# Sigmoid attention and skip-MoE on one core: v's shared rows loaded once, the first expert chosen a batch earlier, gates behind the count, an aligned loop

## The chip, the cores and the metric

The kernel runs on one core of a Trainium2 chip. The metric is the device time of one execution in microseconds. The engines are TensorE (PE; PEld is its weight load), VectorE (DVE), ScalarE (ACT), GpSimd (POOL) and SyncE (SP, which issues most of the DMAs). Every engine works through its own instructions in the order in which they were written; semaphores make it wait for others.

## The reference

q, k and v have the shape (8, 12, 448, 64): B=8 batches, 12 heads, 448 positions, 64 elements a head. Attention's output is the input of a mixture of experts with N = 3584 tokens of 768 elements, 8 experts and a hidden width of 1024. Tokens whose skip score is not above zero pass unchanged.

```python
scores = scale * np.matmul(q, k.transpose(0, 1, 3, 2)) - np.log(S)
attn = 1.0 / (1.0 + np.exp(-scores))
x = np.matmul(attn, v).transpose(0, 2, 1, 3).reshape(B * S, H * D)
do_compute = x @ w_skip > 0
xc = x[do_compute]
logits = xc @ w_gate
e_idx = np.argmax(logits, axis=1)              # one expert a token
probs = softmax(logits)                        # with 1e-9 in the denominator
gate_w = probs[np.arange(len(xc)), e_idx]
for e in range(8):                             # mask: the tokens of expert e
    h = np.maximum(xc[mask] @ w1[e], 0.0)
    y[mask] = gate_w[mask, None] * (h @ w2[e])
out = x.copy()
out[do_compute] = xc + y
```

## The kernel before

**Attention** is 48 steps (b, hp): eight batches by six pairs of heads; n counts the steps. A step has four chunks c: three of 448 columns and, for c=3, one of 224. For each chunk PE makes the scores (s<-x, line 217), ACT the sigmoid (at<-s, line 237), and PE the product with v (pa<-at,v, line 245). The products stand two chunks behind the scores in PE's order, so values(n, c=3) stands in step n+1 at c=1.

**What feeds it.** Every second step loads the k and q of two steps (load_kq, line 177), and v for two steps (load_v, line 191). v's rows come in seven chunks of 64. The upper 64 partitions of a v tile hold chunks 0 to 3, the lower 64 chunks 3 to 6: chunk 3 is loaded twice. k and q are loaded once with a shift; four POOL copies (other_part, line 184) at c=0 of every even step n make the shifted part for steps n+2 and n+3. DVE's two transposes (prep, line 202) at c=0 and c=1 turn them into the x of the next step. For the first step alone, kq_first is loaded with both parts by DMA, on SP and ACT.

**What leaves it.** Step n's sum is added and turned by DVE (lines 255 and 260) and stored by SP (line 268).

**Routing** of batch b-1 runs beside the attention of batch b: logits at hp=0, route at hp=1, the six gate instructions (lines 352 to 358) at hp=2, c=1, ahead of the second transpose. route_count at hp=2, c=3 counts the tokens before each token (matmuls pc, then DVE lines 375 to 389) and leaves four puts, kept in a list `due`: POOL scatters of 112 tokens' records into each expert's list (line 394). They are taken from the list at hp=3 (two), and at hp=4 between the kq copies (two).

**The first expert.** choose_first, at step (B-5, hp=3), takes the expert with most tokens so far (three batches counted). From step W0 = N-26 on, its weights come in 28 pieces through seven buffers wr (line 456), how_many pieces in each step. One step later wsplit makes of each piece a high part on DVE (wh, line 465) and a low part on POOL (wl, line 466).

**The experts.** Behind attention the first 256 tokens of the first expert are computed (names b_ph, b_py), and DVE works out a plan of the remaining blocks. A runtime loop (line 1493) reads the kind of the next block and branches into one of four arms, which stand in the order FULL, FEW, HALF, SPLIT. FEW takes up to 32 tokens and HALF up to 64, with raw weights; SPLIT is a full block that also splits the next expert's raw weights. While a block runs, SP loads the raw weights of the next expert (lines 1176 and 1185). Each pass ends with a POOL scatter of its tokens (line 550). In the trace 14 passes ran, the first a SPLIT and the last a FEW.

The order of the instructions is written by hand (tc.manual_schedule). The chosen first expert and the plan are decided at run time from the data.

Of the kernel before, what the change touches and what calls it, by code (L numbers as in the profile page):

```python
# [23 lines left out]
def kernel(  # L24
# [161 lines left out]
    def load_v(b, hp, n):  # L186

        x = io.tile([P, 2 * n, NV, D], F32, tag="v", name=f"v_{b}_{hp}", bufs=2)
        a = v[b, 2 * hp : 2 * (hp + n)]
        for m in range(2):  # L190
            nc.sync.dma_start(
                x[m * D : (m + 1) * D].rearrange("p h c d -> p h (c d)"),
                a.rearrange("h (p c) d -> p h (c d)", c=NR7)[:, :, 3 * m * D : (3 * m + NV) * D],
            )
        return x

    def prep(b, hp, t, xs=None):
# [10 lines left out]
    def scores(b, hp, c, xs):  # L208

        sc = new_s(f"s_{b}_{hp}_{c}")
        for m in range(2):
            first, qs = (4 * m + c, slice(0, S)) if c < 3 else (3, slice(m * HQ, (m + 1) * HQ))
            for j in range(2):
                r = slice(j * D, (j + 1) * D)
                nc.tensor.matmul(  # L217
                    sc[m * D : (m + 1) * D, j, : qs.stop - qs.start],
                    xs[r, 0, first::NR7],
                    xs[r, 1, qs],  # L220
                    start=True,
                    stop=True,
                )
        return sc
# [135 lines left out]
    def route_count(b, rec):  # L360
# [5 lines left out]
        for s in range(1, NC + 1):  # L366
# [13 lines left out]
        )  # L380

        nc.vector.scalar_tensor_tensor(
            pos, pos, -OOB, hb[:, :NC], op0=ALU.add, op1=ALU.mult
        )
        nc.vector.tensor_tensor(base, base, pc[:, n:m], op=ALU.add)
        sel = sm.tile([P, NC], F32, tag="sel", name=f"sel_{b}", bufs=1)
# [176 lines left out]

    W0 = N - 26
    how_many = (1, 1, 1, 1, 1, 2) * 4
    order = tc.manual_schedule()
# [5 lines left out]
    for n in range(2):  # L572
        for h, eng in enumerate((nc.sync, nc.scalar)):
            load_kq(kq0, 0, 0, slice(0, 1), range(ND), (n,), (h,), eng)
    kq = {0: new_kq(0, 0)}
    load_kq(kq[0], 0, 0, slice(1, 2), range(1))

    warm = const.tile([P, 1], F32, name="warm")
    nc.scalar.activation(warm, bias, AF.Sigmoid)
    vs = {0: load_v(0, 0, 2)}  # L580
    kq[1] = new_kq(*steps[2])
# [44 lines left out]
    xts, lts, rts, sgs = {}, {}, {}, {}  # L626
    wrs = []

# [16 lines left out]
    for n, (b, hp) in enumerate(steps):  # L645
# [39 lines left out]
        for c in range(4):  # L685
# [3 lines left out]
            if c == 0 and n % 2 == 0 and n + 2 < N:  # L689
                for g in range(2):  # L690
                    other_part(kq[n // 2 + 1], g)
                    if due and hp == 4 and b < B - 1:
                        due.pop(0)()
            if c == 0 and nxt:
# [8 lines left out]
            if c == 1:  # L703
                if hp == 2 and b > 0:
                    gates(pb, rts[pb])
                if nxt:
# [4 lines left out]
                if n % 2 == 0 and n + 2 < N:  # L711
                    vs[n // 2 + 1] = load_v(*steps[n + 2], 2)
            if c == 1 and n == N - 2:

# [7 lines left out]
            if c == 2:  # L722
                if hp == 3 and b == B - 5:
                    choose_first()
# [6 lines left out]

            if due and hp == 3 and (c % 2 if b < B - 1 else c < 2):
                due.pop(0)()
# [9 lines left out]
            if c == 3 and hp == 2 and b > 0:  # L743
                due = route_count(pb, rts[pb][0])
                if b == B - 1:
                    for _ in range(2):
                        due.pop(0)()
# [3 lines left out]
            if c == 3 and hp == 2 and b > 0:  # L751
                if pb == B - 2:
                    close_first()
        wrs = wrs_next
        xs = xs_next
# [345 lines left out]
    for j in range(2):  # L1101
        gemm2(j, hh0, hl0, py)
    turn0(1)
    for j in range(2, NK2 - 3):
        gemm2(j, hh0, hl0, py)
# [418 lines left out]
```

## Time and profile before

| what | us |
|---|---|
| runs | 537.68, 531.07, 534.7; median 534.7 |
| profiled execution | 538.86, with a span of 537.2 |
| before the first score of PE | 0 to 7.6 |
| attention | 7.6 to 285.9 |
| first expert's first two blocks (b0, b1) | 285.9 to 325.2 |
| first pass of the loop | 325.2 to 347.9 |
| thirteen more passes | 347.9 to 521.4 |
| behind PE's last matmul | 521.4 to 537.2 |

A row of a view is either a group (engine, line, operation, tiles, count, busy time, mean of one, idle time ahead) or a single run of instructions (start, duration, engine, line, operation, in brackets the idle time ahead and what ended it). An arrow `out<-in` names the tile written and the tiles read. A row of the waits names the waiting engine and line, what it waited for, and then the total, the times and the longest. A row of the chain has start, duration, engine, line.

### The profile page before, as it was taken

The page shows a single profiled execution, that of the slowest core. Times are in us where ns is not written, and L with a number is a line of the kernel's source. Part 1 is how long each engine was busy: PE and PEld are TensorE (multiplying, and loading weights), DVE is VectorE, ACT ScalarE, POOL GpSimd, SP SyncE. Part 2 cuts the span into 40 slices and gives each one's busy share as a digit, 9 for nine tenths or more (in the row PEclk, how much of TensorE's full clock was granted, in tenths as well). Part 3 has the DMA queues.
Part 4 walks back from the last instruction along what each step waited for, and adds up shares of the span by engine and source line. Part 5 has one row for each costly group of instructions (what it writes and reads, how often), then busy time and mean ns, then how long its engine had stood idle before and what let it go on. Part 6 is the DMA issues. An engine that isn't in the chain of part 4 may idle for free.

```text
span 537.2 us, 15241 instructions
## 1 busy us (share of the span) xinstructions
PE 506.3 (94%) x4985; PEld 337.0 (63%) x4986; DVE 296.9 (55%) x732; ACT 274.0 (51%) x483; POOL 259.5 (48%) x413
## 2 busy tenths in 40 slices
PE   7999999999999999999999998999999999999970
PEld 5555555555555555556446986859587878787850
DVE  4555758568586795675856922962213232369321
ACT  3676766767767566666662122922212323177220
POOL 3523554345566874666674140453324444455642
PEclk8999999999999999999999998999999999999995
DMA  7999897798999899998964046688493959595930
GB/s 207 202 232 221 174 200 152 153 185 176 206 207 233 191 212 197 192 224 168 216 111 95 1 128 245 227 246 299 128 380 108 378 165 381 175 393 163 366 75 7
DMA packets 140481, 107.67 MB, mean 200 GB/s; under 512 B 97013, under 2 KB 112795, under 8 KB 140432
## 3 DMA queue, kind: packets, MB, share of 16 engines
q1 hardware_dynamic: 134096, 97.88, 70.0%
q0 software_dynamic: 4576, 8.66, 7.1%
q8 instruction: 31, 0.51, 0.4%
q10 hardware_dynamic: 1760, 0.48, 0.4%
q14 instruction: 18, 0.15, 0.1%
HBM read 98.93 MB, written 17.60 MB: 217 GB/s over the span
## 4 chain that ended last, share of the span: by engine, by line
PE 74%; DMA 9%; DVE 4%; SPq 4%; issue 3%; ACT 2%; POOL 1%; ACTq 0%; POOLq 0%; DVEq 0%
PE s L217 16%; PE pa L245 14%; PE ph L496 12%; PE py L523 11%; DMA out_dram<-y 4%; PE b_ph L496 3%; PE b_py L523 3%; PE py L1347 3%; PE ph L1347 3%; SPq L268 2%; PE pxt L472 2%; PE py L1414 2%; PE ph L1414 2%; DVE x L202 1%; DMA wr<-in_moe_w_dram 1%
## 5 line engine op out<-in xcount | busy, mean ns | idle before, releaser
L237 ACT ACTIVATE at<-s,bias 128x896 f32<-128x896 f32 x192 | 172.0, 914 | 84.6 <-PE s L217 82.3
L217 PE MATMUL s<-x 64*64 64x448 f32 (+1 forms) x1536 | 166.1, 501 | 7.0 <-DVE x L202 3.3
L245 PE MATMUL pa<-at,v 64*64 64x448 f32 (+1 forms) x1536 | 162.2, 490 | 0.0
L184 POOL COPY kq<-kq 32x896 f32<-32x896 f32 (+1 forms) x96 | 88.2, 919 | 104.6 <-DMA kq<-in_q_dram 62.0
L217 PEld LDWEIGHTS s<-x 64*64 64x64 f32 x1536 | 79.0, 191 | 63.7 <-issue 26.4
L245 PEld LDWEIGHTS pa<-at,v 64*64 64x64 f32 x1536 | 62.0, 133 | 55.7 <-issue 47.6
L202 DVE STREAM_TRANSPOSE x<-kq 128x448 f32<-128x448 f32 x94 | 83.0, 945 | 13.7 <-POOL kq L184 11.8
L255 DVE TENSOR_TENSOR xt<-xt,pa 128x448 f32<-128x448 f32 x48 | 29.5, 614 | 46.1 <-ACT xt L642 42.3
L394 POOL DMA_INDIRECT lst<-rec,idx x32 | 32.3, 1009 | 18.3 <-issue 10.5
L466 POOL TENSOR_TENSOR wl<-wr,wh 128x384 fp32r<-128x384 f32 (+1 forms) x28 | 31.7, 1143 | 8.9 <-DVE wh L465 7.7
L260 DVE STREAM_TRANSPOSE y<-xt 128x448 f32<-128x448 f32 x48 | 31.0, 646 | 4.4 <-DMA out_dram<-y 2.6
L550 POOL DMA_INDIRECT out_dram<-ys,rp x15 | 23.7, 1578 | 15.8 <-issue 8.2
L505 ACT ACTIVATE hs<-ph 128x512 f32<-128x512 f32 x14 | 8.4, 598 | 43.9 <-PE ph L496 35.9
L523 PE MATMUL py<-wh,hh 128*128 128x384 f32 x112 | 29.8, 346 | 0.0
L516 DVE TENSOR_TENSOR hl<-pht,hh 128x512 fp32r<-128x512 f32 x14 | 9.7, 690 | 36.0 <-ACT hh L515 27.6
L523 PE MATMUL py<-wh,hl 128*128 128x384 f32 x112 | 28.8, 338 | 0.0
L523 PE MATMUL py<-wl,hh 128*128 128x384 f32 x112 | 28.7, 337 | 0.0
L496 PE MATMUL ph<-wh,xh 128*128 128x512 f32 x84 | 26.3, 410 | 2.6 <-issue 2.6
L496 PE MATMUL ph<-wl,xh 128*128 128x512 f32 x84 | 27.2, 410 | 0.0
L482 DVE TENSOR_TENSOR xl<-pxt,xh 128x384 fp32r<-128x384 f32 x30 | 15.3, 552 | 20.7 <-PE py L1347 8.9
L642 ACT ACTIVATE xt<-pa 128x448 f32<-128x448 f32 x48 | 25.7, 536 | 1.9 <-PE pa L245 1.3
L496 PE MATMUL ph<-wh,xl 128*128 128x512 f32 x84 | 25.2, 404 | 0.0
(273 smaller groups left out, 666.9 us busy)
## 6 DMA issues: line engine op xcount, KB each, us to landing
raw<-in_moe_w_dram SPq DMA_DIRECT2D x64, 768.0 KB
v<-in_v_dram SPq DMA_DIRECT2D x48, 256.0 KB
out_dram<-y SPq DMA_DIRECT2D x192, 56.0 KB
kq<-in_k_dram SPq DMA_DIRECT2D x46, 224.0 KB
kq<-in_q_dram SPq DMA_DIRECT2D x46, 224.0 KB
wr<-in_moe_w_dram SPq DMA_DIRECT2D x12, 256.0 KB
wr<-in_moe_w_dram SPq DMA_DIRECT2D x16, 192.0 KB
lst<-fill SPq DMA_DIRECT2D x4, 464.0 KB
```

The costliest lines, as they stand in the source:

```text
L184: nc.gpsimd.tensor_copy(a[BT:, :, :, :BT], a[:BT, :, :, BT:])
L202: nc.vector.transpose(xs[:, n].rearrange("p (r j) -> p j r", j=NJ), t.rearrange("p (j d) -> p j d", d=D)[:, :, :BT],)
L217: nc.tensor.matmul(sc[m * D : (m + 1) * D, j, : qs.stop - qs.start], xs[r, 0, first::NR7], xs[r, 1, qs], start=True, stop=True,)
L237: nc.scalar.activation(at[:, :, :n], sc[:, :, :n], AF.Sigmoid, bias=bias, scale=SCALE)
L245: nc.tensor.matmul(pa[j * D : (j + 1) * D, r, qs], vt[rs, j, r + c if c < 3 else 3 * (1 - r), :], at[rs, j, : qs.stop - qs.start], start=( ...
L255: nc.vector.tensor_tensor(x, x, pa[:, 1, :S], op=ALU.add)
L260: nc.vector.transpose(y, xts[b][:, hp, :])
L394: put = nc.gpsimd.indirect_dma_start(out=lst[:, :], out_offset=bass.IndirectOffsetOnAxis(ap=idx[:, c : c + 1], axis=0), in_=rec[:, c, :], ...
L466: nc.gpsimd.tensor_tensor(lo, r, hi, op=ALU.subtract)
L496: nc.tensor.matmul(ph[h], a[:, j * P : (j + 1) * P], w[j][h], start=(n == 0), stop=(n == len(t) - 1),)
L523: last = nc.tensor.matmul(py[:, o, :H2], a[h][:, js], w[j][:, o * H2 : (o + 1) * H2], start=(j == 0 and n == 0), stop=(j == NK2 - 1 and n ...
L1347: nc.tensor.matmul(dst[g * SM : (g + 1) * SM, :n], a, w, start=(j == 0), stop=(j == most - 1), tile_position=(0, g * SM),)
```

## The change

The parts of the diff, in the order of the code:

1. load_v loads the lower half's chunks 4 to 6 only, and share_v, a POOL copy of 64x4x64 elements, writes chunk 3 into the lower half from the upper. It is called at c=1 of an even step, for the v of that step and the next.
2. The score tile of step (0, 0), chunk 2, takes a buffer of the other PSUM pool.
3. gates is called behind route_count at hp=2, c=3; in route_count the update of base stands ahead of that of pos.
4. W0 is N-32, how_many spreads the 28 pieces over 31 steps, and a piece is split two steps after its load (`held`); the last step splits what is left.
5. kq_first is loaded with its first part only; two ACT and two POOL copies make the other part.
6. The puts go out at hp=3, c=0 and c=1, and at hp=4, c=1 and c=2.
7. choose_first is called a batch earlier: two batches are counted.
8. An alignment of PE's instructions stands in the second of the two first blocks, some way ahead of the loop.

```diff
             nc.sync.dma_start(
-                x[m * D : (m + 1) * D].rearrange("p h c d -> p h (c d)"),
-                a.rearrange("h (p c) d -> p h (c d)", c=NR7)[:, :, 3 * m * D : (3 * m + NV) * D],
+                x[m * D : (m + 1) * D, :, m:].rearrange("p h c d -> p h (c d)"),
+                a.rearrange("h (p c) d -> p h (c d)", c=NR7)[:, :, 4 * m * D : (3 * m + NV) * D],
             )
         return x
+
+    def share_v(x):
+        nc.gpsimd.tensor_copy(x[D:, :, 0], x[:D, :, NV - 1])
...
-        sc = new_s(f"s_{b}_{hp}_{c}")
+        if (b, hp, c) == (0, 0, 2):
+            sc = ps_a.tile([P, 2, 512], F32, tag="a", name="s_third")
+        else:
+            sc = new_s(f"s_{b}_{hp}_{c}")
...
+        nc.vector.tensor_tensor(base, base, pc[:, n:m], op=ALU.add)
         nc.vector.scalar_tensor_tensor(
             pos, pos, -OOB, hb[:, :NC], op0=ALU.add, op1=ALU.mult
         )
-        nc.vector.tensor_tensor(base, base, pc[:, n:m], op=ALU.add)
...
-    W0 = N - 26
-    how_many = (1, 1, 1, 1, 1, 2) * 4
+    W0 = N - 32
+    how_many = (1, 1, 1, 0) * 7 + (2, 3, 2)
...
-            load_kq(kq0, 0, 0, slice(0, 1), range(ND), (n,), (h,), eng)
+            load_kq(kq0, 0, 0, slice(0, 1), range(1), (n,), (h,), eng)
...
+    def first_part(n, h):
+
+        a = kq0[h * D : (h + 1) * D, n, 0].rearrange("p (j d) -> p j d", d=D)
+        return a[BT:, :, :BT], a[:BT, :, BT:]
+
+    for n in range(2):
+        nc.scalar.activation(*first_part(n, 1), AF.Copy)
+        nc.gpsimd.tensor_copy(*first_part(n, 0))
...
                     other_part(kq[n // 2 + 1], g)
-                    if due and hp == 4 and b < B - 1:
-                        due.pop(0)()
...
             if c == 1:
-                if hp == 2 and b > 0:
-                    gates(pb, rts[pb])
                 if nxt:
                     prep(*nxt, part(n + 1)[1], xs_next)
...
+            if c == 1 and n % 2 == 0:
+                share_v(vs[n // 2])
...
-                if hp == 3 and b == B - 5:
+                if hp == 3 and b == B - 6:
                     choose_first()
...
-            if due and hp == 3 and (c % 2 if b < B - 1 else c < 2):
+            if due and (c in (1, 2) and hp == 4 or c < 2 and hp == 3):
                 due.pop(0)()
...
                 due = route_count(pb, rts[pb][0])
+                gates(pb, rts[pb])
...
-        wrs = wrs_next
+        wrs = held + wrs_next if n == N - 2 else held
+        held = wrs_next
...
     turn0(1)
+    nc.tensor.addr_align(bass.FETCH_BLOCK_INSTRUCTIONS, offset=0, max_nops=0)
     for j in range(2, NK2 - 3):
         gemm2(j, hh0, hl0, py)
```

Three places in the order of the instructions. The first is POOL at hp=4 of the sixth batch, an even step: kq_0 is the tile that other_part completes, lst is the records' list that the puts write, wl a weight's low part. Before:

```order
L394 DMA lst<-rec_3100,idx_3216 29696x16
L466 TENSOR_TENSOR wl_3_139<-wr_3131,wh_3_131 128x384 [waits DMAHW0_49,DVE_49]
L394 DMA lst<-rec_3100,idx_3216 29696x16
L184 COPY kq_0_3220<-kq_0_3220 32x2x14x32 [waits DMAHW7_49,DMAHW1_49,Pool_49]
L184 COPY kq_0_3220<-kq_0_3220 32x2x14x32 [waits DMAHW0_49,DMAHW2_49,DMASW5_49,DMASW4_49]
L394 DMA lst<-rec_3100,idx_3216 29696x16 [waits Pool_49]
L184 COPY kq_0_3220<-kq_0_3220 32x2x14x32
L184 COPY kq_0_3220<-kq_0_3220 32x2x14x32 [waits DMASW6_49]
L394 DMA lst<-rec_3100,idx_3216 29696x16 [waits Pool_49]
```

And after, the same step:

```order
L400 DMA lst<-rec_3115,idx_3222 29696x16 x2
L472 TENSOR_TENSOR wl_2_138<-wr_3070,wh_2_130 128x384 [waits DMAHW6_49,DVE_49]
L184 COPY kq_0_3234<-kq_0_3234 32x2x14x32 [waits DMAHW4_49,DMAHW2_49,Pool_49]
L184 COPY kq_0_3234<-kq_0_3234 32x2x14x32 [waits DMAHW3_49,DMAHW5_49,DMASW5_49,DMASW4_49]
L184 COPY kq_0_3234<-kq_0_3234 32x2x14x32 x2
L198 COPY v_4_3179<-v_4_3179 64x4x64 [waits PE_49,Pool_49]
L400 DMA lst<-rec_3115,idx_3222 29696x16
L472 TENSOR_TENSOR wl_2_138<-wr_3144,wh_2_130 128x384 [waits DVE_49,Pool_49]
L400 DMA lst<-rec_3115,idx_3222 29696x16
```

The puts left their places between the copies and stand behind them; the new copy of v's shared rows (line 198) stands right behind the four.

The second place is PE at the end of an even step's values, in the second batch. pa_0 is the sum of step n (hp=0), s_1 the scores of step n+1. Before:

```order
L217 MATMUL s_1_1_1169<-x_1_1069 64x448 [waits DVE_49,PE_49]
L217 MATMUL s_1_1_1169<-x_1_1069 64x448 x3
L245 MATMUL pa_0_1101<-at_0_3_1106,v_0_962 64x224 x4
L217 MATMUL s_1_2_1185<-x_1_1069 64x448 [waits Activation_49]
L217 MATMUL s_1_2_1185<-x_1_1069 64x448 x3
```

And after:

```order
L223 MATMUL s_1_1_1176<-x_1_1075 64x448 [waits DVE_49,PE_49]
L223 MATMUL s_1_1_1176<-x_1_1075 64x448 x3
L251 MATMUL pa_0_1108<-at_0_3_1113,v_0_961 64x224 x2
L251 MATMUL pa_0_1108<-at_0_3_1113,v_0_961 64x224 [waits Pool_49]
L251 MATMUL pa_0_1108<-at_0_3_1113,v_0_961 64x224
L223 MATMUL s_1_2_1192<-x_1_1075 64x448 [waits Activation_49]
```

Nothing moved, but the third of the four matmuls now waits for POOL, and the next step's scores stand behind it.

The third place is DVE at hp=2 of the second batch: x_3 is the next step's tile, om and sume belong to the gates, pos, base, sel and idx to the count. Before:

```order
L202 STREAM_TRANSPOSE x_3_1238<-kq_2_996 128x14x32 [waits PE_49,Pool_49]
L352 TENSOR_SCALAR om_1256<-sg_1221 128x32 [waits Activation_49]
L353 RECIPROCAL om_1256<-om_1256 128x32 [waits DVE_49]
L354 TENSOR_TENSOR om_1256<-om_1256,sg_1221 128x32 [waits DVE_49]
L356 TENSOR_REDUCE sume_1260<-om_1256 128x4 [waits DVE_49]
L357 TENSOR_SCALAR sume_1260<-sume_1260 128x4 [waits DVE_49]
L358 RECIPROCAL rec_1198<-sume_1260 128x4 [waits DVE_49,Pool_49]
L202 STREAM_TRANSPOSE x_3_1238<-kq_2_996 128x14x32
L255 TENSOR_TENSOR xt_1057<-xt_1057,pa_1_1191 128x448 [waits Activation_49]
```

And after:

```order
L205 STREAM_TRANSPOSE x_3_1245<-kq_2_1002 128x14x32 [waits PE_49,Pool_49]
L205 STREAM_TRANSPOSE x_3_1245<-kq_2_1002 128x14x32
L261 TENSOR_TENSOR xt_1063<-xt_1063,pa_1_1198 128x448 [waits Activation_49]
L266 STREAM_TRANSPOSE y_1_1265<-xt_1063 128x448 [waits DMAHW6_49,DMAHW1_49,DMAHW7_49,DMAHW0_49,DVE_49]
L381 TENSOR_TENSOR pos_1304<-pc_1298,base 128x32 [waits PE_49]
L388 TENSOR_TENSOR base<-base,pc_1298 128x8 [waits DVE_49]
L389 SCALAR_TENSOR_TENSOR pos_1304<-pos_1304,hb 128x32
L393 TENSOR_REDUCE sel_1308<-pos_1304 128x4 [waits DVE_49]
L395 TENSOR_SCALAR idx_1310<-sel_1308 128x4 [waits DVE_49]
L358 TENSOR_SCALAR om_1312<-sg_1228 128x32
```

The six gate instructions left their place between the two transposes and now begin behind idx.

More of the change, by code (lines that the diff above doesn't have):

```diff
@@ L626 @@
     xts, lts, rts, sgs = {}, {}, {}, {}
-    wrs = []
+    wrs, held = [], []
     line = []
```

## The prediction

> **What bounds the kernel now.** I read the page's busy shares first, then the span cut into stages, then the chain, then the waits inside each stage.
>
> ```profile
> PE 506.3 (94%) x4985; PEld 337.0 (63%) x4986; DVE 296.9 (55%) x732; ACT 274.0 (51%) x483; POOL 259.5 (48%) x413
> ...
> core 0: us, PE busy (x) PEld busy (x) DVE busy (x) ACT busy (x) POOL busy (x), PEclk, DMA share, GB/s
> 7.60:130.40 122.80, 122.62 (x1551) 65.37 (x1555) 79.22 (x159) 85.85 (x111) 54.44 (x65) 0.99 0.93 193
> 130.40:285.90 155.50, 149.88 (x1937) 84.44 (x1933) 107.67 (x229) 103.65 (x136) 101.14 (x110) 1.00 0.92 193
> 325.20:347.90 22.70, 20.14 (x101) 17.74 (x102) 13.44 (x23) 13.66 (x26) 7.71 (x12) 0.92 0.77 279
> 347.90:521.40 173.50, 170.23 (x1160) 131.06 (x1160) 67.93 (x191) 59.80 (x185) 78.85 (x183) 1.00 0.75 252
> 521.40:537.20 15.80, 0.00 (x0) 0.00 (x0) 1.76 (x7) 1.15 (x2) 3.51 (x9) 0.58 0.06 11
> ```
>
> TensorE (PE) is the bound: 94% of the span. Each stage row gives its length and then PE's busy time, so the difference is all that a change of order can win there: 0.18 us in the first half of attention, 5.62 in the second, 2.56 at the entry of the expert loop (at a clock of 0.92), 3.27 in the later passes. The DMA engines stand at 0.93 and 0.92 in attention: nearly full, so that loads land late without PE waiting for them yet. No matmul goes away, so the sum below is a sum of waits. The profiled execution took 538.86 us, 4.2 above the median of the runs (534.7); I sum against it and then take 4.2 off.
>
> **The start.** Before attention PE has no real work:
>
> ```profile
> 2.24 4.20 DMA kq_first<-in_q_dram
> ...
> 6.64 0.94 DVE x L202
> ...
> 7.63 2.62 PE s L217 x13
> ```
>
> Eight loads of kq_first become four, two on each of two queues. The last was issued at 2.24 and took 4.20 us; it is now the second on its queue, about 0.9 earlier. Behind it comes a new copy on ACT; the nearest row is ACT's copy of 128x448 in 536 ns.
>
> ```profile
> L642 ACT ACTIVATE xt<-pa 128x448 f32<-128x448 f32 x48 | 25.7, 536 | 1.9 <-PE pa L245 1.3
> ```
>
> So 0.9 less 0.54 is 0.4 gained; if the halved bytes also land a microsecond sooner, 1.4. I take **−0.9**, between these. The third score tile in another PSUM buffer (s_third) only spares PE a wait that the 0.18 us of the next stage bounds: nothing.
>
> **Stalls removed in the second half of attention.** What PE waited for there:
>
> ```profile
> PE s L217 <- DVE x L202: 3.3, 5, 1.2
> DVE wh L465 <- DMA wr<-in_moe_w_dram: 10.8, 8, 3.0
> ...
> 193.16 1.04 PE L217 MATMUL s<-x 64*64 64x448 f32 x8 [0.32 <-DVE x L202]
> 195.35 0.67 PE L217 MATMUL s<-x 64*64 64x448 f32 x4 [0.40 <-DVE sel L387]
> 211.17 0.67 PE L217 MATMUL s<-x 64*64 64x448 f32 x4 [1.23 <-DVE x L202]
> ```
>
> The columns of the first two are total, times, longest. The 1.23 at 211 us is DVE standing in front of a weight split whose load had not landed. Splitting two steps after the load instead of one takes that away. The 0.32 and 0.40 at 193–195 are the six gate instructions between DVE's two transposes of the next step, and the order of base and pos; moved behind the count they delay nothing that PE waits for in that chunk. Two later batches show the like, so I count 1.23 + 0.72 + 0.6, **−2.6**; the bounds are −1.2 (the weight wait alone) and −3.7 (all of the 3.3 and the 0.40). The other 2 us of idle time wait for late loads and y stores. The 28 weight pieces now go over 31 steps, before over 24, which thins the traffic and may give some back; I put that under the next term.
>
> **The new wait: v's shared rows.** share_v is queued on POOL behind the four kq copies of the even step, and PE's third matmul of values(n, c=3) now waits for it. In before nobody needed those copies so soon. What the copies wait for, and when they ran, beside that group of matmuls (64x224) in the same step:
>
> ```profile
> POOL kq L184 <- DMA kq<-in_q_dram: 62.0, 23, 8.2
> POOL kq L184 <- DMA lst<-rec,idx: 22.8, 13, 3.1
> SPq L191 <- PE pa L245: 8.4, 5, 4.2
> ...
> 14.16 3.87 POOL L184 COPY kq<-kq 32x896 f32<-32x896 f32 x4 [4.69 <-DMA kq<-in_q_dram]
> 15.83 0.55 PE L245 MATMUL pa<-at,v 64*64 64x224 f32 x8
> 56.47 3.87 POOL L184 COPY kq<-kq 32x896 f32<-32x896 f32 x4 [6.85 <-DVE x L202]
> 59.90 0.56 PE L245 MATMUL pa<-at,v 64*64 64x224 f32 x8
> 240.86 0.92 POOL L184 COPY kq<-kq 32x896 f32<-32x896 f32 x1 [2.27 <-DMA kq<-in_q_dram]
> 242.57 0.59 PE L245 MATMUL pa<-at,v 64*64 64x224 f32 x8
> 255.82 2.90 POOL L184 COPY kq<-kq 32x896 f32<-32x896 f32 x3 [0.38 <-DMA kq<-in_q_dram]
> 254.64 0.56 PE L245 MATMUL pa<-at,v 64*64 64x224 f32 x8
> ```
>
> The third matmul is 0.2 us into its group. The copies end at 18.03 against 16.0, 60.34 against 60.1, and 258.72 against 254.8. At 240.86 four copies without the puts between them (the change takes the puts out) would end near 244.8 against 242.8. share_v moves 256 elements where a copy moves 896 in 0.92 us: bounded by 0.26 and 0.92, I take 0.4. So the four steps would make PE wait 2.4, 0.6, 2.4 and 4.3 us: 2.4 on average. Behind the waiting matmul stand all of PE's scores; ACT, DVE and the y stores then wait for PE.
>
> How often it is paid is the question. A wait moves PE back against the DMA queues, so the next loads are less late; v loads that wait for PE (the SP row, 5 times) hand a delay on to the loads behind them. The lower end is **+1**: the shared rows are no longer loaded, 64 KB in each of 24 loads, 1.57 MB or 8 us at the stage's 193 GB/s, and with the thinner weights this eats most of the lateness. The upper end is **+20**: 2.4 us in 8 of the 23 even steps. I take **+6**: the first wait (2.4) and later the largest (4.3), less some relief.
>
> **Entry of the loop.**
>
> ```profile
> 327.77 0.47 PE L496 MATMUL ph<-wh,xh 128*128 128x512 f32 x1 [2.56 <-issue]
> ...
> 327.77 8.08 PE ph L496 x27
> ...
> 469.53 6.50 PE ph L496 x27
> L1488 PEldq COMPARE_BRANCH  x8: 73/194/3435, 324.2 to 484.8; - x8
> q8 instruction: 1, 0.02, 2.0%
> ...
> q14 instruction: 1, 0.01, 0.0%
> ```
>
> The first pass was a SPLIT block, whose arm lies behind the three others. One branch took 3435 ns where the median is 194, an instruction fetch (q8) stands in that window, and PE idled 2.56 us; then 27 matmuls took 8.08 instead of 6.50. That is 2.56 + 1.58 = 4.1. In the window of all later passes q8 has no packet. I counted the reference's tokens by expert (36, 12, 0, 158, 17, 675, 19, 416) and followed the planner's arithmetic with them. With two batches counted instead of three the first expert becomes 5 instead of 7, and the 14 passes, SPLIT first before, become FULL, FULL, HALF, SPLIT, and so on: the same number of each kind. The first pass falls straight into its arm, which begins behind the loop's head. **−4.1**, bounds 0 and −4.1.
>
> The Trainium skill ("Runtime: NRT & Kernel Launch", Instruction fetch mechanics) says that a taken branch outside the two-page window forces a fetch before execution goes on. By that rule every later jump to another arm would stall too; the trace disagrees, having none in the later passes, but it cannot tell whether the first jump to SPLIT, now in pass four, will pay.
>
> The same skill ("TensorE: Matmul & The Clock Gate", Part 1) gives half clock only after an idle window of about 3.4 us; the row had 2.56 us idle and still a clock of 0.92 after it. By the rule the gain would be 2.6, and the sum 1.5 higher.
>
> **The tail.** By the same arithmetic the new order ends FEW, then HALF, two small experts in a row; before, FEW was the last, behind a SPLIT.
>
> ```profile
> 461.87 2.73 PE ph L1347 x48
> 378.67 5.30 PE ph L1414 x24
> ...
> 390.90 3.23 PE ph L496 x13
> ...
> q1 hardware_dynamic: 2684, 6.29, 84.8%
> ...
> 518.47 4.00 PE py L1347 x32
> 526.73 1.41 POOL L550 DMA_INDIRECT out_dram<-ys,rp  x1 [0.60 <-issue]
> 393.22 1.50 POOL L550 DMA_INDIRECT out_dram<-ys,rp  x1 [0.58 <-issue]
> ```
>
> A pass's raw weights (6.29 MB) load while the pass ahead runs. FEW at 461.87 lasts 7.66 (to 469.53), but the loads (the q1 row is of the window from 464.6 to 484.6) land until 22.7 us after its start. A HALF behind it, 12.23 long when dense (378.67 to 390.90), would end 19.9 after FEW's start; held by its last weights it ends near 25: +5.3 (bounds +3 and +6.5). Against it, the last scatter starts 5.35 after a FEW's last matmul (521.4 to 526.73) but 2.3 after a HALF's (390.90 to 393.22): −3.0. Net **+2.3**, bounds 0 and +4.
>
> **Sum.** 538.9 − 0.9 − 2.6 + 6 − 4.1 + 2.3 = 539.6; less 4.2 is **535**. A measurement of this kernel tells about 2%, 10.7 us, from no change: 524 and 545.4.
>
> **Rivals.**
> - The copy is in time. For it: step 8 is late by only 0.6, and both relieving edits work on every step. Against: copies late by 4 us at 258 with the queues at 0.92. With +1 for +6: **530**. 30%.
> - The wait is paid again and again, slower than before. The place is PE's third matmul of c=3, the price 2.4 us a time. It decides once a delay of PE delays SP's next v and kq loads by as much, for then nothing catches up. For it: the SP row, and copies that wait 62 us in all for their loads, 23 times. Against: 5 waits in 48 steps, and idle queue time to catch up in. With +20: **549**. 12%.
> - The fetch is not avoided but moved to pass four, so that the entry does not do what the new order suggests. For it: SPLIT is still behind three arms. Against: no fetch in later passes. With 0 for −4.1: **539**. 10%. The Trainium skill's rule on taken branches, above, speaks for it.
> - My forecast holds 45%; 3% for something else.
>
> The best of all terms (−1.4 − 3.7 + 1 − 4.1 + 0) would be −8.2, 526. I give 526 to 547: what is left out is most of the repeated wait, and gains that I have no row for. Faster by over 2% needs more than the best terms: 6%. Slower by over 2% is the repeated wait at near its full price: 11%. Within: 83%.
>
> **What would show it.** PE's first score near 6.7 us instead of 7.63; a row of PE pa waiting for POOL's v copy, some 6 us in all, with its longest near 4 (nothing: first rival; 20 in many pieces: second); no DVE wait for wr longer than 3 in front of a PE gap; no gap of 2.5 at the loop's entry and a first pass whose first 27 matmuls take 6.5; a PE wait of about 5 us for raw weights in the last pass, and a scatter 2.3 behind its last matmul. I am wrong if kq loads land in another place than now, since the whole new wait hangs on them, or if the changed split order holds DVE elsewhere.

## The result, and the profile after

The changed kernel is slower: 551.2 us (550.0 to 553.1, 4 runs) against 533.9 (531.1 to 537.7, 4 runs), a ratio of 1.0328 (95% interval 1.0286 to 1.037). The prediction was 535, with a range of 526 to 547: wrong. Its profiled execution took 550.01 us with a span of 548.0, 10.8 more than before's span. Of one kernel below (share_v ahead of the kq copies) three of ten executions were slow ones, the profiled one of 544.9 us among them: its ratio leaves them out, its median does not.

First the stages. The rows of after, by the windows that match those of before (steps 0 and 1; steps 2 to 25; steps 26 to 46; the last step; the two first blocks). Columns: length, then the busy time of PE, PEld, DVE, ACT, POOL, then PE's granted clock, the DMA share and GB/s.

```profile
6.30:20.70 14.40, 11.65 (x112) 7.22 (x116) 6.69 (x20) 7.30 (x9) 9.05 (x14) 0.88 0.84 194
20.70:157.90 137.20, 136.37 (x1749) 89.04 (x1745) 86.91 (x179) 95.44 (x124) 67.99 (x83) 1.00 0.89 189
157.90:278.00 120.10, 118.99 (x1512) 71.32 (x1508) 82.82 (x179) 83.68 (x110) 75.82 (x88) 1.00 0.88 186
278.00:290.00 12.00, 7.73 (x125) 4.62 (x117) 8.62 (x12) 4.68 (x7) 9.95 (x11) 1.00 0.57 123
290.00:330.80 40.80, 40.80 (x225) 35.77 (x226) 24.53 (x114) 8.54 (x21) 12.53 (x16) 0.96 0.21 56
```

And the same stages of before:

```profile
7.60:18.80 11.20, 11.17 (x112) 5.59 (x116) 6.11 (x19) 7.32 (x9) 6.03 (x9) 0.85 1.07 236
18.80:153.00 134.20, 134.06 (x1747) 72.51 (x1743) 87.80 (x176) 94.58 (x124) 60.84 (x70) 1.00 0.91 189
153.00:277.40 124.40, 119.48 (x1516) 67.45 (x1508) 90.42 (x189) 82.63 (x110) 81.75 (x86) 1.00 0.94 200
277.40:285.90 8.50, 7.80 (x121) 4.26 (x121) 2.57 (x6) 4.97 (x7) 6.96 (x10) 1.00 0.54 102
285.90:325.20 39.30, 39.30 (x224) 34.41 (x224) 24.30 (x114) 8.43 (x21) 10.70 (x12) 1.00 0.23 61
```

The start is 1.3 us shorter (6.3 against 7.6). Then 3.2 are lost in the first two steps, 3.0 in steps 2 to 25 (only 0.8 of it idle time of PE), and 4.3 won in steps 26 to 46, where the DMA share fell from 0.94 to 0.88. At the last step attention is even with before. After that 3.5 are lost in the last step and 1.5 in the first blocks, whose clock is 0.96; the rest, 5.2, is lost in the loop and behind it.

The two rows of the first two steps hide something. Both show a reduced clock, but in different places (before, then after; window, length, busy time of PE alone, its clock, DMA share, GB/s):

```profile
8.40:11.80 3.40, 3.40 (x24) 0.50 1.08 241
...
17.00:20.40 3.40, 3.40 (x28) 0.51 0.20 37
```

In before PE ran 3.4 us at half clock right behind its wait of 1.96 us for the first scores. In after that stretch is gone (clock 1.00 up to 16 us), and one of the same length stands behind the wait for the copy, which ended at 16.26. So the copy cost more than the difference of the two rows says: with the copy moved ahead (below) step 2 starts at 15.9 instead of 20.7.

The waits of PE in the profile after say where (total, times, longest):

```profile
PE ph L1430 <- DMA raw<-in_moe_w_dram: 6.1, 2, 3.4
PE pa L251 <- POOL v L198: 4.7, 4, 2.8
PE b_px L478 <- DVE xt L261: 4.3, 1, 4.3
PE ph L502 <- issue: 3.0, 1, 3.0
```

Four rows, four places: the last pass waits for raw weights, attention for the copy of v's shared rows, the first expert's first block for DVE, and one pass of the loop for nothing that the list of waits shows. The wait of DVE for wr is gone from the list, and so are PE's waits for DVE x. The chain of after around the loop's entry and its end:

```profile
327.69 3.15 PE b_py L529 x18
330.83 6.30 PE ph L502 x27
...
341.81 7.40 PE py L529 x42
349.21 2.96 issue
352.17 7.81 PE ph L502 x27
...
505.21 2.73 PE ph L1363 x48
...
511.34 8.78 DMA raw<-in_moe_w_dram
...
520.25 8.00 PE ph L1430 x22
...
529.80 5.40 PE py L1430 x32
...
537.50 1.49 POOL out_dram L556
```

No gap at the entry (330.83 follows 327.69 directly, and 27 matmuls take 6.30), but one of 2.96 between the first pass and the second, with 7.81 for the 27 matmuls behind it: the same price, one pass later. The trace names the place. The branch of `tc.If` on line 1499, by which PE leaves the arm FULL for the loop's end behind the three others, was slow once, like the branch at the entry in before (shortest, median, longest in ns):

```profile
L1499 PEldq COMPARE_BRANCH  x15: 68/193/4582, 329.5 to 503.4; - x15
```

An instruction block (q8) was loaded then: one packet between 347 and 353 us, and none from 353 to 535. The slow branch begins at 345.9 and ends at 350.5; the packet lies ahead of 349.2, to which the matmuls ran on and where the idle time begins.

The last pass starts HALF's matmuls 10 to 15 us behind the start of FEW (505.21), waits for the raw load to 520.1, and runs 22 matmuls in 8.00 us.

### The profile page after: what moved, and what is told of

It is laid out like the page before. It is cut to its first block, busy times and chain, and to the rows that moved or that the text cites. A ratio compares the mean times of both kernels' runs of the same rounds, so it can differ in the third digit from the quotient of the medians.

```text
span 548.0 us, 15275 instructions
## 1 busy us (share of the span) xinstructions
PE 514.3 (94%) x4985; PEld 363.4 (66%) x4986; DVE 295.7 (54%) x732; ACT 277.0 (51%) x485; POOL 269.5 (49%) x439
## 4 chain that ended last, share of the span: by engine, by line
PE 80%; DMA 8%; DVE 3%; POOL 3%; issue 3%; SPq 2%; ACT 1%; POOLq 0%; ACTq 0%; DVEq 0%
PE pa L251 18%; PE s L223 18%; PE ph L502 11%; PE py L529 11%; PE b_ph L502 3%; DMA lst<-rec,idx 3%; PE b_py L529 3%; PE ph L1363 3%; PE ph L1430 2%; PE py L1363 2%; PE pxt L478 2%; PE py L1430 2%; PE pl L283 2%; DMA raw<-in_moe_w_dram 2%; DMA kq<-in_q_dram 2%
## 5 line engine op out<-in xcount | busy, mean ns | idle before, releaser
L243 ACT ACTIVATE at<-s,bias 128x896 f32<-128x896 f32 (+1 forms) x191 | 171.6, 914 | 83.1 <-PE s L223 80.7
L251 PE MATMUL pa<-at,v 64*64 64x448 f32 (+1 forms) x1536 | 186.8, 493 | 4.7 <-POOL v L198 4.7
L223 PE MATMUL s<-x 64*64 64x448 f32 (+1 forms) x1528 | 184.6, 498 | 0.1
L223 PEld LDWEIGHTS s<-x 64*64 64x64 f32 x1528 | 97.4, 191 | 39.9 <-issue 14.2
L251 PEld LDWEIGHTS pa<-at,v 64*64 64x64 f32 x1536 | 80.3, 134 | 56.9 <-issue 38.6
L205 DVE STREAM_TRANSPOSE x<-kq 128x448 f32<-128x448 f32 x94 | 81.8, 945 | 8.1 <-POOL kq L184 6.1
L1244 POOL TENSOR_TENSOR xn<-xn,zf 128x1 f32<-128x1 f32 x14 | 5.2, 373 | 40.0 <-PE pxt L478 40.0
```

Source lines behind the costliest of these rows:

```text
L205: nc.vector.transpose(xs[:, n].rearrange("p (r j) -> p j r", j=NJ), t.rearrange("p (j d) -> p j d", d=D)[:, :, :BT],)
L223: nc.tensor.matmul(sc[m * D : (m + 1) * D, j, : qs.stop - qs.start], xs[r, 0, first::NR7], xs[r, 1, qs], start=True, stop=True,)
L243: nc.scalar.activation(at[:, :, :n], sc[:, :, :n], AF.Sigmoid, bias=bias, scale=SCALE)
L251: nc.tensor.matmul(pa[j * D : (j + 1) * D, r, qs], vt[rs, j, r + c if c < 3 else 3 * (1 - r), :], at[rs, j, : qs.stop - qs.start], start=( ...
```

## The experiments

Each ratio is to the kernel before, measured beside it on the same chip, since the medians of before differ by up to 0.8% from chip to chip (534.0, 537.1, 538.4 and 536.6 in the four sets). Between sets, ratios are compared. After's own ratio is 1.0328.

**The first expert, by force.** Only the choice is replaced.

```diff
-        nc.vector.tensor_scalar(hot0, cnt, cm, None, op0=ALU.is_equal)
+        nc.vector.memset(cm, 1.0)
+        nc.vector.tensor_scalar(hot0, desc, cm, None, op0=ALU.is_equal)
```

> The changed kernel, with expert 7 set as the first expert by a constant (it is the one that before chose from three batches); all else as changed. The order of passes is then that of before: SPLIT first, FEW last. Theory A (the loss is in four places: 5.8 us in the tail, about 5 at the last attention step, 4.7 at the first steps, and the jump's fetch moved to pass two without gain): the last pass's wait for raw weights (6.1) and its slow clock (2.7) go, the scatter comes 3 later behind a FEW; the fetch is paid at the entry again. 551.2 - 5.8 = 545. Rival B (the repeated wait for v's shared rows makes the loss): 550 to 552, since attention is the same.

Measured: 535.36 us, 1.0038 (0.9993 to 1.0083). Some 15.5 us come back (0.029), far more than the 5.8 of the tail, and rival B falls. In the profile PE's waits for raw weights and for "issue" are both gone:

```profile
PE pa L251 <- POOL v L198: 5.8, 5, 2.7
...
PE b_px L479 <- DMA x<-out_dram,rp: 1.1, 1, 1.1
```

The expectation was wrong about the entry. It put the fetch back there; the chain shows none, and the 27 matmuls take 6.64:

```profile
324.93 3.15 PE b_py L530 x18
328.08 6.64 PE ph L503 x27
```

So a SPLIT block first costs no fetch here, where before it cost 2.56 us. And the 4.3 at b_px went to 1.1 although the splits are the same. Both are followed up below.

**The last step without splits.** One piece in each of 28 steps:

```diff
-    how_many = (1, 1, 1, 0) * 7 + (2, 3, 2)
+    how_many = (1,) * 28
```

> The changed kernel with one weight piece in each of 28 steps instead of 1,1,1,0 seven times and then 2,3,2: the last steps of attention load none, and the last step splits none. Theory A: the DVE row of five splits of 6.1 us in the last step goes, with it PE's 4.3 us wait for DVE at b_px and the slow clock behind it (1.5): 551.2 - 4.8 = 546.4. Rival B: denser loads before make the wait for v's shared rows longer: 551 to 554.

Measured: 547.6 us (1.0262, 1.0195 to 1.0328), 3.6 less than after, but the interval overlaps after's (1.0286 to 1.037). The profile is what tells: the wait at b_px fell from 4.3 to 0.2, and the later waits for the shared rows are larger (1.45, 1.13 and others of 0.8), as the rival had it. Both theories hold for their part.

**The first v pair loaded whole.**

```diff
-    vs = {0: load_v(0, 0, 2)}
+    vs = {0: load_v(0, 0, 2, True)}
...
-            if c == 1 and n % 2 == 0:
+            if c == 1 and n % 2 == 0 and n > 0:
                 share_v(vs[n // 2])
```

> The changed kernel, but the v of the first two steps is loaded with its shared rows as before, and the copy of shared rows begins with the second pair. Theory A: PE's wait in step 1 (2.8 us, and 1.9 of slow clock) goes: 551.2 - 4.7 = 546.5. Rival B (a wait that is removed comes back two steps later, since the queues are full): a wait of 2 to 3 us stands at step 3 or 5, 549 to 551.

Measured: 547.98 us (1.0276, 1.020 to 1.0352), 3.3 less, again with an interval that overlaps after's. In the profile step 2 starts at 16.7 instead of 20.7 and the last step at 274.1 instead of 278.0, and no wait for the copy over 0.45 us is left in all of attention: the wait did not come back two steps later.

**Without the alignment.**

```diff
-    nc.tensor.addr_align(bass.FETCH_BLOCK_INSTRUCTIONS, offset=0, max_nops=0)
```

> The changed kernel without the alignment of PE's instructions. Theory A: a fetch is paid once in any case where the code first jumps over the arms; it stays at the end of the first pass or at its start: 551.2, within 1.5. Rival C (the alignment pushed the loop's end out of what is fetched ahead): no gap of 3 us at pass two and no slow clock behind it, 551.2 - 4.3 = 547.

Measured: 550.9 us (1.0322, 1.0255 to 1.0389), no change; the gap at pass two is 2.92. With a FULL block first the alignment makes no difference that these runs can see. With expert 7 forced it does:

> Expert 7 set as the first expert (535.4 us, where no gap stood at the loop's entry), now without the alignment of PE's instructions. Theory A (the alignment is worth the entry's fetch when a SPLIT block comes first): a gap of about 2.5 at the entry and 27 first matmuls of about 8: 535.4 + 4 = 539.5. Rival C (the alignment does nothing, another edit moved the code into place): 535.4 within 1.

Measured: 543.6 us, 1.0128 (1.0089 to 1.0167), against 1.0038 with the alignment. The chain of this kernel has the gap at the entry:

```profile
334.27 3.16 PE b_py L530 x18
337.44 2.13 issue
339.57 6.54 PE ph L503 x27
```

That is 2.1 of its 4.8 us more; no slow clock followed here. This execution (548.9 us, 5 above the median) also had waits of 4.0 at b_px and 2.4 for the copy of v's rows, which are not at the entry; the rest of the 4.8 is not explained. And the alignment alone, in the kernel before:

```diff
     turn0(1)
+    nc.tensor.addr_align(bass.FETCH_BLOCK_INSTRUCTIONS, offset=0, max_nops=0)
     for j in range(2, NK2 - 3):
```

> The kernel before with one edit of the change alone: the alignment of PE's instructions ahead of the loop. Theory A: the gap of 2.3 to 2.6 at the entry and the slow clock behind it (up to 1.6) go: 0.993. Rival C (the place of the code depends on everything ahead, and before's is another): the gap stays, 1.000.

Measured: 534.5 against 538.4 us, 0.9936 (0.9913 to 0.9959). The first pass follows at once:

```profile
321.34 3.15 PE b_py L523 x18
324.49 6.56 PE ph L496 x27
```

So the alignment is worth what the entry costs, 0.6%, where a SPLIT block comes first, and rival C falls for this case. A slow branch of PE goes with the gap in every profile: 3.0 to 3.4 us at the entry in the three kernels with SPLIT first and no alignment (before, its second profile, and this one with expert 7), 4.5 to 4.8 at the end of FULL in all that begin with FULL, and none over 0.6 us in those with SPLIT first and the alignment.

**The stall at b_px.** In the profile after, one of DVE's five casts of the last step takes 4.5 us where the others take 0.35. Beside it POOL's rows (start, duration, then the group):

```profile
L471 DVE CAST wh<-wr x5: 343/348/4515, 283.3 to 284.9; 128x384 fp32r<-128x384 f32 x5
284.23 1.09 POOL L546 DMA_INDIRECT x<-out_dram,rp  x1 [0.28 <-POOL x L695]
285.34 3.85 POOL L472 TENSOR_TENSOR wl<-wr,wh 128x384 fp32r<-128x384 f32 x4
289.33 0.61 DVE L261 TENSOR_TENSOR xt<-xt,pa 128x448 f32<-128x448 f32 x1
```

The first has min, median and longest. The fifth cast starts at 284.9 and ends with POOL's fourth subtraction. In the kernel with expert 7 forced POOL began 1.7 us later and the casts were through:

```profile
L472 DVE CAST wh<-wr x5: 341/348/969, 284.6 to 286.3; 128x384 fp32r<-128x384 f32 x5
287.05 4.89 POOL L473 TENSOR_TENSOR wl<-wr,wh 128x384 fp32r<-128x384 f32 x5
```

To test it, POOL's five subtractions were written in reverse order in the last step, so that the first waits for DVE's last cast:

```diff
-                    for w in wrs:
-                        wsplit(*w)
+                    if n == N - 1:
+                        for r, hi, lo in wrs:
+                            nc.vector.tensor_copy(hi, r)
+                        for r, hi, lo in reversed(wrs):
+                            nc.gpsimd.tensor_tensor(lo, r, hi, op=ALU.subtract)
+                    else:
+                        for w in wrs:
+                            wsplit(*w)
```

> The changed kernel, but in the last attention step POOL's five subtractions (a weight's low part) are written in reverse order, so that the first of them waits for DVE's fifth cast; the work is the same. Theory A (DVE's cast of 4.5 us stands still while POOL subtracts without a break, 285.3 to 289.2): all casts take 0.3 to 1, PE's wait at b_px falls from 4.3 to about 1 and the slow clock behind it goes: 551.2 - 4.6 = 546.6. Rival E (the cast waits for its load): the last cast still ends near 289, no change.

Measured: 547.9 us, 1.0183 (1.0134 to 1.0232). By the ratios that is 0.0145 or 7.8 us less, more than the 4.6 expected; the difference is not explained. The casts, and PE at b_px:

```profile
L743 DVE CAST wh<-wr x5: 341/348/986, 287.9 to 289.6; 128x384 fp32r<-128x384 f32 x5
291.19 0.85 PE L478 MATMUL b_px<-ident,x 128*128 128x128 f32 x6 [0.48 <-DMA x<-out_dram,rp]
```

The same loads, the same work, and no long cast: the load did not hold it, so rival E falls. The last step is back at before's length: 8.6 us (282.6 to 291.2) against 8.5. The Trainium skill ("SBUF — State Buffer", Who interferes with whom) says that a DVE instruction in a two-port mode and a POOL instruction take one pair of ports in turn, and that the second to issue blocks fully. The rows agree that the cast stood still beside POOL's work: it lasted until the fourth subtraction ended, and 0.35 us where POOL left it alone. That this cast runs in such a mode no row shows. Nor does the rule explain the length: the cast began at 284.9, behind POOL's transfer of 284.23 but ahead of the first subtraction of 285.34, and four subtractions went ahead of its end. Why is not in the rows.

**A second profile of before.**

> The kernel before, unchanged, for a second profile, since its first one (538.9) lay 4.9 above the median of its runs (534.0). Theory A: its attention waits for late loads and stores (5.6 us of idle PE in the second half) change from one execution to the next, and this one has 1 to 3 us of them; the 2.56 us gap at the loop's entry is in the code and stands again. Rival D: the entry's gap itself is there in some executions only, and is what spreads the runs of before from 530 to 538.

Measured: 537.18 us, with 535.5 of span. The gap at the entry is 2.3; attention's second half (130.4 to 285.9) has 5.8 us of idle PE against 5.6 in the first profile, not 1 to 3. Neither theory found what spreads the runs of before. One difference shows, though: in the first profile PE ran at half clock for 3.4 us at the start and again behind the entry's gap, and in the second neither (the 27 matmuls behind the gap took 6.54, not 8.08). By estimate half a clock for 3.4 us costs 1.7 us, so the two are worth about 3.4 of the 4.9 us by which the first profile lay above the median.

**The place of share_v.** The copy stands ahead of the kq copies:

```diff
+            if c == 0 and n % 2 == 0:
+                share_v(vs[n // 2])
             if c == 0 and n % 2 == 0 and n + 2 < N:
                 for g in range(2):
                     other_part(kq[n // 2 + 1], g)
...
-            if c == 1 and n % 2 == 0:
-                share_v(vs[n // 2])
```

> The changed kernel, but share_v stands on POOL ahead of the step's four kq copies instead of behind them; the copy itself, its bytes and everything else stay. Theory A (PE waits for the queue place, that is for the kq loads that the copies ahead wait for): no PE wait for POOL's v copy over 0.5 us in any step, and no slow clock in step 1: the ratio to before falls by about 0.012 from the changed kernel's 1.033 (4.7 of waits and 1.9 of slow clock), to 1.021. Rival B' (PE would wait at the same places for late kq or x instead): waits of DVE x or POOL kq take the place, 1.030 or more.

Measured: a median of 542.7 us against 538.4, and a ratio of 1.0051 (1.0014 to 1.0088). No PE wait for the copy is left, nor in the three later kernels with the copy in this place. The last step starts at 270.5 us, where in after it starts at 278.0: 7.5 us of attention. (In the later kernel that has this edit and reversed subtractions, it starts at 271.4.) The ratio fell by 0.028 or 15 us, where 0.012 was expected; what the other half is, this profile does not show, and the kernel's runs spread from 536.7 to 545.8. The copy itself and its neighbours, at the first pair:

```profile
8.11 0.39 POOL L198 COPY v<-v 64x256 f32<-64x256 f32 x1 [0.41 <-DMA v<-in_v_dram]
12.05 3.87 POOL L184 COPY kq<-kq 32x896 f32<-32x896 f32 x4 [3.55 <-DMA kq<-in_q_dram]
```

In after the copy ran at 15.81, behind the four. The wait was the place in the queue, not the copy of 0.39 us.

**Three batches again.** Four kernels take the first expert's choice, W0 and how_many back to before, keep the split two steps behind the load and reverse the last step's subtractions. The first has the first v pair loaded whole:

```diff
-    W0 = N - 32
-    how_many = (1, 1, 1, 0) * 7 + (2, 3, 2)
+    W0 = N - 26
+    how_many = (1, 1, 1, 1, 1, 2) * 4
...
-                if hp == 3 and b == B - 6:
+                if hp == 3 and b == B - 5:
```

> The changed kernel with the first expert chosen from three batches as before (W0 and how_many as before too, the split still two steps behind the load), the first v pair loaded whole, and the last step's subtractions reversed. All other edits stay. Theory A: expert 7, SPLIT first, FEW last, no gap at the entry (aligned), no wait in the first steps: 535.4 - 4.1 - 1 = 530, 0.993 of before. Rival B (the waits for v's shared rows come back under the denser weight loads of 24 steps): 534 to 538.

Measured: 535.8 us, 0.9972 (0.9947 to 0.9998), worse than theory A: the profile has waits of 2.5, 1.3 and 0.6 us for the copy of the shared rows, as rival B said. With share_v ahead of the kq copies instead:

> First expert from three batches as before, share_v ahead of the kq copies from the first pair on, last step's subtractions reversed, all other edits as changed (aligned). Theory A: no wait of PE for the v copy, no fetch at the entry, no wait for raw weights at the end: 0.997 (that kernel with share_v behind the copies and the first pair loaded whole) less 5 us of waits, 0.988. Rival B': the waits come back as late kq loads or y stores, 0.995 to 1.0.

Measured: 531.1 us, **0.9855** (0.9822 to 0.9888): 1.5% faster than before. And with the shared rows loaded twice, as before, and no share_v:

> The same kernel, but v's shared rows are loaded twice as before and there is no share_v. Theory A (the 1.57 MB are worth little while the queues have time left): within 0.003 of the kernel with share_v ahead, 0.988. Rival F (the bytes saved are what keeps loads from being late): 0.993 to 0.998, with PE waiting for DVE x in the second half of attention.

Measured: 533.5 us, 0.9898 (0.9864 to 0.9933). PE's wait rows, first with share_v ahead, then without:

```profile
PE s L223 <- DVE x L205: 1.8, 3, 0.9
```

```profile
PE s L223 <- DVE x L205: 3.5, 5, 1.7
```

The direction is that of rival F, but the size lies between the two (0.0043 behind, where theory A allowed 0.003 and rival F began at 0.0075), and the two intervals overlap: the 1.57 MB are worth some 0.4% or nothing.

**The choice by itself, and the gates.** The changed kernel with both mended places, the choice from two batches kept:

> The changed kernel with both mended places (share_v ahead of the kq copies, last step's subtractions reversed), but the first expert still chosen from two batches, over 31 steps. It differs from the best kernel so far (0.9855) in that choice and its weights' spread alone. Theory A: the fetch stands at pass two (2.9 and 1.3 of slow clock), the last HALF pass waits 6 us for raw weights and runs at a slow clock, its scatter comes 2 to 3 sooner: 10 to 12 us more, 1.005 to 1.008. Rival G (most of the 15.9 us that the forced expert gave back was the stall of the cast, which is gone here): 0.993 or less.

Measured: 540.8 against 536.6 us, 1.0073 (1.0042 to 1.0103). Against 0.9855 with three batches the choice, with the spread of its weights over 31 steps, costs 2.2%, some 11.7 us, as theory A had it. The two places found in the profile of after, 4.3 us at pass two and 7.1 at the tail (worked out below), make 11.4. Two rows carry it:

```profile
PE ph L1436 <- DMA raw<-in_moe_w_dram: 6.2, 2, 5.6
PE ph L502 <- issue: 3.0, 1, 3.0
```

> The best kernel so far, but the gates stand at hp=2, c=1 ahead of the second transpose again, as before. Theory A: PE waits for DVE x at step hp=2 of most batches by 0.3 to 0.6 us, some 1.3 to 2 in all: 0.9855 + 0.003, 0.989. Rival H (with the loads on time DVE has room, and the place of the gates does not matter): 0.9855 within 0.002, no PE wait for DVE x at hp=2.

The edit:

```diff
+                if hp == 2 and b > 0:
+                    gates(pb, rts[pb])
                 if nxt:
                     prep(*nxt, part(n + 1)[1], xs_next)
...
                 due = route_count(pb, rts[pb][0])
-                gates(pb, rts[pb])
```

Measured: 531.4 us, 0.9886 (0.9847 to 0.9925). That is theory A's figure, but the interval also holds rival H's, so the time does not decide. The trace has theory A's waits, in two batches: 0.89 us at 90.62 and 0.17 at 124.89, each at the first scores behind hp=2, with the gates between DVE's two transposes (DVE, DVE, PE):

```profile
86.81 0.62 DVE L358 TENSOR_SCALAR om<-sg 128x32 f32<-128x32 f32 x1
...
89.57 0.91 DVE L205 STREAM_TRANSPOSE x<-kq 128x448 f32<-128x448 f32 x1
90.62 1.04 PE L223 MATMUL s<-x 64*64 64x448 f32 x8 [0.89 <-DVE x L205]
```

In the kernel with the gates behind the count the same scores start without a wait, at 89.92. In the second half of attention PE does not wait for DVE x at all here. So the gates ahead cost 1.1 us of waits in this execution; whether moving them is worth time is not shown.

## Why the prediction was wrong, point by point

**Where it started from.** The sum was made on a profiled execution of 538.9 us, 4.2 above the median, and ended at +0.7. On that scale the change brought 11.2 (550.0); on the medians 17.3. The 6.1 us between are the two profiled executions: before's lay 4.9 above the median of its runs, after's 1.2 below. Some 3.4 of the 4.9 are the two stretches at half clock, which the second profile of before does not have; why before's other runs are shorter is not shown. On the scale of the spans, what changed adds up so: start −1.3, steps 0 to 46 +1.9, last step and first blocks +5.0, entry +0.1, tail +7.1, the other passes −2.0 (PE's four waits of 0.5 for ACT in the FEW passes are gone), together +10.8.

**The start**: −0.9 predicted, −1.3 measured; right. The half clock in before's first steps belongs to the one execution, since the second profile of before does not have it; no term stood for it.

**The stalls removed**: −2.6. Steps 26 to 46 got 4.3 shorter in the profile, more than the bound of −3.7. PE's waits for DVE x and sel, 3.7 us in before, are all gone, and so is DVE's wait for wr. Which edit did it is not isolated: the gates ahead cost 1.1 us of waits in the last kernel above, and the thinner traffic (share 0.94 to 0.88) works in the same direction.

**The new wait**: +6 predicted. PE waited 4.7 us for the copy: 2.8 of it in step 1, with a clock of 0.51 in the 3.4 us from 17.0, then 0.8, 0.9 and 0.2. Moved ahead it gave 7.5 us back by the last step. The size was about right, and the first place too; the late wait of 4.3 that the forecast counted on did not come, and the half clock behind the first made up for it. That the sum came out is partly luck. The rival of a wait that is paid every time did not come true: four waits, not eight. That its 549 is close to the measured time is chance.

**Entry of the loop**: −4.1 predicted, +0.1 measured. This is the first step that failed. The prediction let the stall go because the first pass falls into its arm. It went only to the end of that pass: 2.96 and 1.3 of slow clock behind it, against 2.56 and 1.58. The rival "moved to pass four" had the mechanism but the wrong place: the jump out of FULL, over the three other arms, came ahead of any jump into SPLIT. The Trainium skill's rule on taken branches ("Runtime: NRT & Kernel Launch", Instruction fetch mechanics), by which that rival stood, agrees with this: one branch at the end of FULL took 4.6 us where the median is 0.19. Its two-page window is not what the later passes show, as q8 has no packet in them. The prediction gave the alignment no term at all; in fact the alignment removes the whole entry cost when the first block is a SPLIT, and the new choice made it useless by putting FULL first.

**The tail**: +2.3 predicted. HALF's last matmul ended 30.0 us behind the start of FEW (505.21 to about 535.2), not 25; the scatter then followed 2.3 behind it, as said. Against the 19.9 of two dense passes that is +10.1, less 3.0, so the tail was +7.1. (25 less 19.9 is 5.1; the prediction has 5.3.) The step that failed is "held by its last weights it ends near 25": I let the matmuls run piece by piece behind their loads. In the trace 22 of the 24 ph matmuls stand behind the raw load that ends at 520.1, 14.9 after FEW's start; only then come ph, the transposes and py, 15 us in a row, 3.1 of it because a slow clock follows the wait (8.00 us for 22, where before 24 took 5.30). The loads were also issued later: SP's first one 4.3 us behind the start of FEW (509.50), where in before it was 1.7 (463.54 and 461.87). What held it is not isolated.

**What had no term**: the last step's five splits. The diff shows them (2, 3, 2 and the last step splitting what is left). I priced the splits by the weight wait they removed and not by what they bring to the last step, where POOL's subtractions stand beside DVE's casts and DVE's addition stands behind them. It cost 3.5 us at b_px and 1.5 in the slow clock behind it.

The range was too narrow because every term was bounded by itself, and of the three large misses (last step 5.0, tail 4.8, entry 4.2) one had no term and one was counted as a gain. The clock was left out of all waits but one: in the profile of after, slower matmuls worth 1 to 3 us followed in each of the four places with a wait of 2.7 us or more.

## What to carry to other kernels

A new consumer turns a queue's order into a critical path: before a copy goes behind others on an engine, look at what those wait for, and put it ahead where its own input is there long before. A choice at run time (the first expert) sets the order of everything behind it, so its price is read at the far end (which block is last, what loads beside it), not at the place where it is made. A wait of 2 us or more on PE may be followed by a stretch at half clock, 1.3 to 3 us here, which belongs in the range of the forecast though it does not come every time.

## What the runs showed of the hardware

- A DVE cast of 128x384 took 4.5 us beside four POOL subtractions in a row, 0.35 as a rule; the order of POOL's instructions alone took this away. Five profiled kernels had the stall at b_px (4.0 to 4.3 us); the one with expert 7 forced, with the same casts and subtractions in the same order, had not.
- A branch of PE over other arms, with an instruction block loaded beside it, took 3.0 to 4.8 us once in an execution and cost 2.1 to 3.2 us of idle PE, at the entry or at the end of the first pass; the median of the same line is 0.19. With a SPLIT block first, an alignment some instructions ahead hid it (0.9936).
- PE's granted clock fell to half for 3.4 us, or two or three times that, behind some waits: 1.96 us at the start of before, 2.56 at its loop's entry, 2.75, 2.96 and 4.27 in after. Behind others it stayed at 1.00: 2.15 with expert 7 and no alignment, 2.3 in the second profile of before, but also 2.97 at 16.5 us in the kernel without the alignment and 3.50 at 213 us in before with it. So the length of a wait alone does not decide it here. The Trainium skill ("TensorE: Matmul & The Clock Gate", Part 1) gives half clock after at least one idle window of about 3.4 us; the waits of 1.96 to 2.96 here were shorter and slowed the clock all the same, and one of 3.50 did not.
